# Attention over memory slots and two ReLU² MLPs on one core: the float64 weight conversion leaves GpSimd, and its first two pieces move to the front

## The chip, the cores and the metric

One core of a Trainium2 chip runs the whole program. The metric is the device time of one execution in microseconds (us), as the median of several runs. The engines are called PE (TensorE, matrix products; PEld is its weight load), DVE (VectorE), ACT (ScalarE), POOL (GpSimd) and SP (SyncE, which here issues nearly all DMAs).

## What is computed

Three stages follow one another: an attention whose keys and values are first pooled into 32 memory slots per head, and two MLPs with a squared ReLU.

```python
def _attn_ref(q, k, v, phi):                 # 8 batches, 8 heads, 576 tokens, 64 wide; phi: 32 slots
    a = np.exp(phi - np.max(phi, axis=2, keepdims=True))
    a = a / (np.sum(a, axis=2, keepdims=True) + 1e-09)
    k_m = np.einsum('bhsm,bhsd->bhmd', a, k)
    v_m = np.einsum('bhsm,bhsd->bhmd', a, v)
    scores = (1 / sqrt(64)) * np.matmul(q, k_m.transpose(0, 1, 3, 2))
    attn = softmax of scores over the 32 slots
    return np.matmul(attn, v_m)

def _moe_ref(x, w_in, w_out, s, b):          # x: 4608 x 512, w_in: 512 x 2048, w_out: 2048 x 512
    g = s * np.maximum(x @ w_in, 0.0) ** 2 + b
    return g @ w_out

def _moe2_ref(x, w_in, w_out):
    return np.maximum(x @ w_in, 0.0) ** 2 @ w_out
```

The four weight matrices (w_in1, w_out1, w_in2, w_out2) arrive as float64; all else is float32.

## The kernel before

**Order of the work.** Batch 0's attention runs first and alone. Then a list of steps `(b, half, f)` drives the first MLP: for one half batch (288 tokens) and one block `f` of 128 hidden units, `h1` makes the hidden block (6 products into `hps`, line 455, then ReLU, square and a high part `g[0]` on ACT, and the low part `g[1]` on DVE, line 464), two steps ahead of `x1`, which multiplies it by w_out1 (12 products into `acc`, line 472). The steps of one (b, half) share one accumulator; `SEGS` begins with batch 0's blocks 0 to 3, then 4 to 7, then batch 1's 0 to 7. Attention of the next batches and `v_fold` (slot values times w_in1, `vps`, line 424, split into high and low parts `vp` on lines 429 and 430) are generators that are advanced between the products. After the last batch a second phase computes the second MLP.

**Split operands.** Products that need more precision than one float32r pass are made of high and low parts: (high, high), (high, low), (low, high). So `x1` needs `g[0]`, `g[1]` and both parts of its piece of w_out1, and waits for the low part of w_out1 with the third product of each column block.

**The float64 conversion.** `narrow_later` lists pieces of 1024 KB: in the order two of w_in1 (kind "float"), two of w_out1 (kind "split"), and so on, 16 in all for the first MLP; the 16 of the second are of kind "spill" and come later. `narrow_load` issues a piece's DMA into a pool `w64` of two buffers (tile `wt`), with a lower priority for the scheduler than the code around it. `narrow` converts a piece of 128x1024 words: on ACT `wx` = high word as a float, scaled (line 119); on DVE a shift by 3 (line 120); for kind "float" ACT makes the sign (line 122), DVE puts the low word's top bits in (line 126) and POOL multiplies by the sign into the tile `w1` (line 129); for the other kinds DVE puts in the sign bit (line 124) and the low bits (line 126); "split" then has a high part on ACT (line 131) and a low part as a subtraction on POOL (line 132). Calls of `narrow` stand at three places of batch 0's attention (`FIRST`) and then at listed steps.

**Batch 0's attention.** `load_phi` and `load_kv` bring phi, k and v. DVE reduces phi to a maximum per partition (line 194, `pm`); two transposes on PE (lines 207, 216) with a reduction and a copy on DVE between them (lines 210, 213) spread it; DVE subtracts (line 221), ACT takes the exponential (line 223, `e`). `kvs` (line 239) is the pooled k and v; for batches 0 and 1 the sum of the weights is one small product per weight tile with `ones` (line 249), for the later batches DVE sums first (line 232, `es`) and two products follow (line 258). Then come the reciprocal `rs` (lines 267, 268), the scaled copies (lines 276, 277), transposes `kvt`, copies into `kb` (line 289), query transposes `qps` (line 305) and copies `qT`, scores `sp` (line 320), the softmax on DVE and ACT (lines 332 to 343: maximum `m_`, subtraction, exponential on ACT, sum `l_`, reciprocal, multiplication), transposed probabilities `pp` (line 348) and their high and low parts `pt` (lines 357, 358).

A scheduler orders each engine's instructions from priorities; each engine then runs its own in that order and waits on semaphores.

## Time and profile before

| | us |
|---|---|
| median of 3 runs | 1603.72 (1602.5 to 1604.74) |
| the profiled execution, its own time | 1603.0 |
| its span in the trace | 1601.2 |
| PE busy in the span | 1559.0 (97%) |
| ACT busy | 703.9 (44%) |
| DVE busy | 676.6 (42%) |
| POOL busy | 40.5 (3%) |

The shares are averages over very different stretches: of the 40 equal slices of the span, PE has 0.5 and 0.8 in the first two and 0.9 or more from the fifth on, while DVE is at 0.9 in the third. The profiled execution lies 0.7 us below the median of the runs and 1.8 us above its own span.

### The profile page before, as it was taken

Reading aid. Unit: us, or ns where it says so; the run is one execution under the profiler, and the core shown is the slowest. Engines: PE = TensorE matmul, PEld = TensorE weight load, DVE = VectorE, ACT = ScalarE, POOL = GpSimd, SP = SyncE. Lnnn points to the kernel's source line nnn. Section 1 sums busy time; section 2 is a strip of 40 time slices with the busy share of each in tenths; the row PEclk is TensorE's granted clock in tenths of the full one; section 3 lists DMA queues with packets and bytes.
Section 4 is the critical chain, followed back from the end, with each engine's and each line's share of the span. In section 5 each row is a group of like instructions: output and inputs, shape, how many; then the busy total and the mean of one; then the engine's idle time right before and its main releaser. Section 6 shows DMA issues by size and latency. Waiting matters only on the chain.

```text
span 1601.2 us, 25941 instructions
## 1 busy us (share of the span) xinstructions
PE 1559.0 (97%) x10872; PEld 1351.6 (84%) x10872; DVE 676.6 (42%) x1155; ACT 703.9 (44%) x1475; POOL 40.5 (3%) x23
## 2 busy tenths in 40 slices
PE   5889999999999999999999999999999999999998
PEld 3778899989999998989988888888888888888887
DVE  5796454645555564444253323232323223232222
ACT  3676555665666666567542322232222222232221
POOL 1323000000000000000000000000000000000000
PEclk8899999999999999999999999999999999999999
DMA  8655322425334441104040102010100101010100
GB/s 270 202 167 176 118 76 66 138 80 174 104 129 124 145 138 45 51 18 145 16 134 27 53 0 53 1 53 0 36 18 4 50 0 53 1 27 0 27 1 27
DMA packets 105300, 118.06 MB, mean 74 GB/s; under 512 B 42208, under 2 KB 82144, under 8 KB 105184
## 3 DMA queue, kind: packets, MB, share of 16 engines
q1 hardware_dynamic: 104864, 115.89, 23.4%
q8 instruction: 85, 1.39, 0.4%
q10 hardware_dynamic: 320, 0.52, 0.1%
q14 instruction: 31, 0.25, 0.1%
HBM read 86.77 MB, written 29.62 MB: 73 GB/s over the span
## 4 chain that ended last, share of the span: by engine, by line
PE 91%; DVE 4%; DMA 2%; ACT 1%; issue 1%; POOL 0%; SPq 0%; ACTq 0%; DVEq 0%
PE hps L676 25%; PE oacc L724 25%; PE acc L472 23%; PE hps L455 12%; PE vps L424 2%; PE sp L320 1%; PE kvs L239 1%; PE qps L305 1%; DMA kv<-in_v_dram 1%; DMA wt<-in_moe_w_out_dram 1%; DVE wx L126 1%; DVE wx L120 1%; PE pp L348 1%; DVE pm L194 1%; DVE wx L124 1%
## 5 line engine op out<-in xcount | busy, mean ns | idle before, releaser
L472 PE MATMUL acc<-g,wo 128*128 128x288 f32 (+1 forms) x3072 | 474.3, 300 | 8.9 <-ACT xo L501 3.4
L472 PEld LDWEIGHTS acc<-g,wo 128*128 128x128 f32 x3072 | 427.8, 190 | 37.7 <-issue 17.1
L724 PE MATMUL oacc<-wo,g 128*128 128x512 f32 x1728 | 419.6, 392 | 0.0
L724 PEld LDWEIGHTS oacc<-wo,g 128*128 128x128 f32 x1728 | 324.3, 188 | 73.4
L676 PE MATMUL hps<-xh,wi 128*128 128x512 f32 x1152 | 384.2, 394 | 0.0
L681 ACT ACTIVATE r<-hps 128x512 f32<-128x512 f32 x144 | 86.0, 597 | 462.4 <-PE hps L676 462.3
L682 DVE TENSOR_TENSOR r<-r 128x512 f32<-128x512 f32 x144 | 99.7, 692 | 445.8 <-ACT r L681 445.8
L676 PEld LDWEIGHTS hps<-xh,wi 128*128 128x128 f32 x1152 | 216.1, 188 | 49.5
L455 PE MATMUL hps<-pt,vp 128*128 128x288 f32 x1536 | 257.6, 301 | 0.3 <-ACT vp L429 0.3
L464 DVE TENSOR_TENSOR g<-r,g 128x288 fp32r<-128x288 f32 x256 | 125.9, 493 | 252.8 <-ACT g L463 250.4
L455 PEld LDWEIGHTS hps<-pt,vp 128*128 128x128 f32 x1536 | 221.5, 190 | 6.2 <-issue 4.3
L676 PE MATMUL hps<-xl,wi 128*128 128x512 f32 x576 | 225.4, 391 | 0.0
L461 ACT ACTIVATE r<-hps 128x288 f32<-128x288 f32 x256 | 105.4, 412 | 193.0 <-PE hps L455 190.6
L684 DVE TENSOR_TENSOR g<-r,g 128x512 fp32r<-128x512 f32 x144 | 99.6, 692 | 84.5 <-ACT g L683 84.5
L683 ACT CAST g<-r 128x512 fp32r<-128x512 f32 x144 | 89.5, 621 | 94.7 <-DVE r L682 93.6
L676 PEld LDWEIGHTS hps<-xl,wi 128*128 128x128 f32 x576 | 108.1, 188 | 25.1
L462 ACT ACTIVATE r<-r 128x288 f32<-128x288 f32 x256 | 113.8, 444 | 6.9
L463 ACT CAST g<-r 128x288 fp32r<-128x288 f32 x256 | 110.7, 432 | 7.1
L430 DVE TENSOR_TENSOR vp<-vps,vp 128x512 fp32r<-128x512 f32 x64 | 41.6, 685 | 12.4 <-ACT vp L429 12.1
L424 PE MATMUL vps<-w,vmT 64*32 64x512 f32 x512 | 39.3, 615 | 4.8 <-POOL w L129 4.6
L126 DVE SCALAR_TENSOR_TENSOR wx<-wt,wx 128x1024 int32<-128x1024 int32 x32 | 41.1, 1283 | 0.4
L429 ACT CAST vp<-vps 128x512 fp32r<-128x512 f32 x64 | 34.7, 587 | 13.3 <-PE vps L424 12.7
(225 smaller groups left out, 727.5 us busy)
## 6 DMA issues: line engine op xcount, KB each, us to landing
wt<-in_moe_w_in_dram SPq DMA_DIRECT2D x16, 1024.0 KB, 6.3
wt<-in_moe_w_out_dram SPq DMA_DIRECT2D x16, 1024.0 KB, 5.9
q<-in_q_dram SPq DMA_DIRECT2D x72, 128.0 KB, 3.3
x1d<-xo SPq DMA_DIRECT2D x16, 576.0 KB, 3.6
kv<-in_k_dram SPq DMA_DIRECT2D x23, 384.0 KB, 4.9
kv<-in_v_dram SPq DMA_DIRECT2D x23, 384.0 KB, 5.2
out_dram<-oo SPq DMA_DIRECT2D x68, 128.0 KB, 2.3
x<-x1d SPq DMA_DIRECT2D x6, 1024.0 KB, 5.5
```

What stands on the lines that cost most here:

```text
L455: nc.tensor.matmul(hps[:, :NB1], lhsT=w[:, wi], rhs=pt[xi][:, hp, t0:t0 + NB1], start=(i == 0), stop=(i == 5))
L461: nc.scalar.activation(r[:, :NB1], hps[:, :NB1], AF.Relu)
L462: nc.scalar.activation(r[:, :NB1], r[:, :NB1], AF.Square)
L463: st["act"] = nc.scalar.copy(g[0][:, :NB1], r[:, :NB1])
L464: nc.vector.tensor_tensor(out=g[1][:, :NB1], in0=r[:, :NB1], in1=g[0][:, :NB1], op=ALU.subtract)
L472: nc.tensor.matmul(acc[d][:, :n], lhsT=wo1[:, f, wi, d * P:d * P + P], rhs=g[xi][:, :n], start=(first and i == 0), stop=(store is not None ...
L676: nc.tensor.matmul(hps[:, :NB2], lhsT=w[:, wi], rhs=xs[i][xi][:, d], start=(n == 0), stop=(n == 3 * ND - 1))
L681: nc.scalar.activation(r, hps[:, :NB2], AF.Relu)
L682: nc.vector.tensor_tensor(out=r, in0=r, in1=r, op=ALU.mult)
L683: nc.scalar.copy(g[0], r)
L684: nc.vector.tensor_tensor(out=g[1], in0=r, in1=g[0], op=ALU.subtract)
L724: nc.tensor.matmul(acc[t], lhsT=g[xi][:, t * P:t * P + P], rhs=wo2[:, f, wi], start=(f == 0 and n == 0), stop=(f == NF - 1 and n == 2))
```

## The change

- Kind "float" no longer uses ACT's sign and POOL's multiplication: DVE puts in the sign bit as for the other kinds, and the instruction that puts in the low bits writes the result straight into `w1`. Kind "split" makes its low part on DVE instead of POOL.
- The DMAs of the first two pieces (both of w_in1) are issued at normal priority: the first right behind phi's, the second behind k and v and ahead of q. The calls of `narrow` in batch 0's attention stand at the generator's steps 4, 8 and 20 instead of 6, 12 and 22.
- Batch 0's weight sums go over DVE's `es` and two products, as for batches 2 and up; batch 1 alone keeps the small products.
- Batch 1's maximum over phi (`pm`) is ordered behind a low part `g[1]` of the first steps (`issue_after(st["dve"])`).

```diff
-    def narrow_load(n=1):
+    def narrow_load(n=1, later=30):
         for src, kind, dst in [narrow_todo.pop(0) for _ in range(min(n, len(narrow_todo)))]:
-            with tc.high_priority(-30):
+            with tc.high_priority(-later) if later else ExitStack():
...
                 nc.vector.tensor_scalar(out=x, in0=x, scalar1=3, scalar2=None, op0=ALU.logical_shift_left)
-                if kind == "float":
-                    nc.scalar.activation(dst[0], hw.bitcast(F32), AF.Sign)
-                else:
-                    nc.vector.scalar_tensor_tensor(out=x, in0=hw, scalar=-(1 << 31), in1=x,
-                                                   op0=ALU.bitwise_and, op1=ALU.bitwise_or)
-                nc.vector.scalar_tensor_tensor(out=x, in0=lw, scalar=29, in1=x,
+                nc.vector.scalar_tensor_tensor(out=x, in0=hw, scalar=-(1 << 31), in1=x,
+                                               op0=ALU.bitwise_and, op1=ALU.bitwise_or)
+                nc.vector.scalar_tensor_tensor(out=dst[0].bitcast(I32) if kind == "float" else x,
+                                               in0=lw, scalar=29, in1=x,
                                                op0=ALU.logical_shift_right, op1=ALU.bitwise_or)
-                if kind == "float":
-                    nc.gpsimd.tensor_tensor(out=dst[0], in0=xf, in1=dst[0], op=ALU.mult)
-                elif kind == "split":
+                if kind == "split":
                     nc.scalar.copy(dst[0], xf)
-                    nc.gpsimd.tensor_tensor(out=dst[1], in0=xf, in1=dst[0], op=ALU.subtract)
-                else:
+                    nc.vector.tensor_tensor(out=dst[1], in0=xf, in1=dst[0], op=ALU.subtract)
+                elif kind == "spill":
                     nc.sync.dma_start(dst[0], xf)
...
-        nc.vector.tensor_reduce(
-            out=pm.rearrange("p (n m) -> p n m", m=M),
-            in_=ph.rearrange("p n j m -> p n m j"), axis=AX.X, op=ALU.max)
+
+        with tc.issue_after(st["dve"].ins) if b == 1 else ExitStack():
+            nc.vector.tensor_reduce(
+                out=pm.rearrange("p (n m) -> p n m", m=M),
+                in_=ph.rearrange("p n j m -> p n m j"), axis=AX.X, op=ALU.max)
...
-            narrow_load(1)
+            narrow_load(1, 0)
...
-            if g == 0 and b > 1:
+            if g == 0 and b != 1:
...
-            if b < 2:
+            if b == 1:
...
-        for hp in range(2 if b > 1 else 0):
+        for hp in range(2 if b != 1 else 0):
...
-        nc.vector.tensor_tensor(out=g[1][:, :NB1], in0=r[:, :NB1], in1=g[0][:, :NB1], op=ALU.subtract)
+        st["dve"] = nc.vector.tensor_tensor(out=g[1][:, :NB1], in0=r[:, :NB1], in1=g[0][:, :NB1], op=ALU.subtract)
...
-    narrow_load(1)
+    narrow_load(1, 0)
...
-        if n in (6, 12, 22) and done < FIRST:
+        if n in (4, 8, 20) and done < FIRST:
```

How the order moves, at three places. Lines of the changed kernel differ: 121 and 123 are the sign bit and the low bits (before 124 and 126), 128 the low part of w_out1 (before 132 on POOL), 192 is `pm`, 208 and 211 the steps between the two transposes, 219 the subtraction, 230 `es`, 265 and 266 `rs`, 287 `kb`, 462 the low part `g[1]`.

SP's queue from the program's start, before:

```order
L169 DMA ph<-in_phi_dram 128x4x288
L178 DMA kv<-in_k_dram 128x4x192
L179 DMA kv<-in_v_dram 128x4x192
L178 DMA kv<-in_k_dram 128x4x192
L179 DMA kv<-in_v_dram 128x4x192
L178 DMA w_3_144<-in_k_dram 128x4x192
L179 DMA w_3_144<-in_v_dram 128x4x192
L185 DMA q<-in_q_dram 128x4x64 x6
L584 DMA s_sb<-in_moe_s_dram 128x1
L585 DMA b_sb<-in_moe_b_dram 128x1
L97 DMA wt<-in_moe_w_in_dram 128x2x512 x2
```

and now:

```order
L165 DMA ph<-in_phi_dram 128x4x288
L97 DMA wt<-in_moe_w_in_dram 128x2x512
L174 DMA kv<-in_k_dram 128x4x192
L175 DMA kv<-in_v_dram 128x4x192
L174 DMA kv<-in_k_dram 128x4x192
L175 DMA kv<-in_v_dram 128x4x192
L174 DMA w_3_144<-in_k_dram 128x4x192
L175 DMA w_3_144<-in_v_dram 128x4x192
L97 DMA wt<-in_moe_w_in_dram 128x2x512
L181 DMA q<-in_q_dram 128x4x64 x6
```

The first piece of w_in1 goes ahead of all six k and v transfers and the second ahead of q's; both were behind all of these, and behind the two small broadcasts.

DVE from the maximum over batch 0's phi on, before (`mx` and `mxb` are the reduction and the copy between the two transposes):

```order
L194 TENSOR_REDUCE pm<-ph 128x128
L210 TENSOR_REDUCE mx<-t_196 128x2
L213 COPY mxb<-mx 128x128
L221 TENSOR_TENSOR ph<-ph,t_202 128x4x96 x3
L267 TENSOR_SCALAR rs<-kvs 128x1 x2
L268 RECIPROCAL rs<-rs 128x2
L289 COPY kb<-kvt 64x4x32 x2
L332 TENSOR_REDUCE m__448<-sp 128x12
L120 TENSOR_SCALAR wx<-wx 128x1024
```

and now, from behind the same maximum:

```order
L120 TENSOR_SCALAR wx<-wx 128x1024
L208 TENSOR_REDUCE mx<-t_196 128x2
L121 SCALAR_TENSOR_TENSOR wx<-wt,wx 128x1024
L211 COPY mxb<-mx 128x128
L123 SCALAR_TENSOR_TENSOR w_0_141<-wt,wx 128x1024
L219 TENSOR_TENSOR ph<-ph,t_202 128x4x96 x3
L230 TENSOR_REDUCE es<-e 128x128
L265 TENSOR_SCALAR rs<-kvs 128x1 x2
L266 RECIPROCAL rs<-rs 128x2
L120 TENSOR_SCALAR wx<-wx 128x1024
L121 SCALAR_TENSOR_TENSOR wx<-wt,wx 128x1024
L287 COPY kb<-kvt 64x4x32
```

The first piece's three DVE instructions now stand between the steps of the maximum, the second piece's around the copies into `kb`; before, both pieces stood behind these, among the softmax.

DVE from behind the low part `g[1]` of the second step, with the third group's softmax, to the low part of the second piece of w_out1, now:

```order
L337 TENSOR_REDUCE l__495<-e 128x12
L338 TENSOR_SCALAR l__495<-l__495 128x12
L339 RECIPROCAL l__495<-l__495 128x12
L120 TENSOR_SCALAR wx<-wx 128x1024
L341 TENSOR_TENSOR e<-e,l__495 128x384
L121 SCALAR_TENSOR_TENSOR wx<-wt,wx 128x1024
L462 TENSOR_TENSOR g_2_158<-r,g_2_157 128x288
L123 SCALAR_TENSOR_TENSOR wx<-wt,wx 128x1024
L356 TENSOR_TENSOR pt_315<-pp,pt_314 128x192
L462 TENSOR_TENSOR g_0_154<-r,g_0_153 128x288
L192 TENSOR_REDUCE pm<-ph 128x128
L128 TENSOR_TENSOR wo_116<-wx,wo_116 128x2x512
```

Before, this low part was POOL's, and batch 1's maximum stood much earlier, behind the first softmax group's multiplication:

```order
L343 TENSOR_TENSOR e<-e,l__456 128x384
L194 TENSOR_REDUCE pm<-ph 128x128
L339 TENSOR_REDUCE l__460<-second 128x12
L358 TENSOR_TENSOR pt_386<-pp,pt_385 128x192
L340 TENSOR_SCALAR l__460<-l__460 128x12
```

The maximum now stands directly ahead of the low part of w_out1, behind the first low parts `g[1]`.

## Rows read from the trace of the kernel before

**Rows 1.** Busy time by stretch: PE, PEld, DVE, ACT, POOL, granted clock, DMA share, GB/s.

```profile
50.00:150.00 100.00, 85.74 (x904) 76.37 (x905) 85.49 (x124) 71.95 (x147) 32.99 (x14) 0.93 0.61 201
150.00:1601.00 1451.00, 1443.71 (x9537) 1253.68 (x9536) 564.17 (x990) 612.00 (x1286) 0.00 (x0) 1.00 0.20 59
```

**Rows 2.** The chain that ended last, from 0 to 60 us: start, length, what.

```profile
26.45 2.21 DVE wx L120
...
30.64 2.53 DVE e L343
...
33.21 0.90 PE pp L348 x3
...
55.12 2.42 POOL wo L132
```

**Rows 3.** POOL's timeline: one of its 16 conversion instructions.

```profile
48.16 2.38 POOL L132 TENSOR_TENSOR wo<-wx,wo 128x1024 fp32r<-128x1024 f32 x1 [15.42 <-ACT wo L131]
```

**Rows 4.** DVE's timeline: instructions with nothing on POOL, and (48.45) one beside POOL.

```profile
24.39 1.22 DVE L126 SCALAR_TENSOR_TENSOR wx<-wt,wx 128x1024 int32<-128x1024 int32 x1
...
38.70 0.68 DVE L120 TENSOR_SCALAR wx<-wx 128x1024 int32<-128x1024 int32 x1
...
40.93 0.35 DVE L358 TENSOR_TENSOR pt<-pp,pt 128x192 fp32r<-128x192 f32 x1
...
48.45 2.41 DVE L464 TENSOR_TENSOR g<-r,g 128x288 fp32r<-128x288 f32 x1 [2.40 <-ACT g L463]
...
51.92 0.44 DVE L464 TENSOR_TENSOR g<-r,g 128x288 fp32r<-128x288 f32 x1
```

**Rows 5.** DVE's groups by line, 20 to 150 us: count | busy us, mean ns | idle before.

```profile
L464 DVE TENSOR_TENSOR g<-r,g 128x288 fp32r<-128x288 f32 x27 | 21.6, 805 | 5.4 <-ACT g L463 5.4
L126 DVE SCALAR_TENSOR_TENSOR wx<-wt,wx 128x1024 int32<-128x1024 int32 x16 | 21.5, 1347 | 0.2
L120 DVE TENSOR_SCALAR wx<-wx 128x1024 int32<-128x1024 int32 x16 | 15.4, 960 | 3.6 <-ACT wx L119 3.6
L124 DVE SCALAR_TENSOR_TENSOR wx<-wt,wx 128x1024 int32<-128x1024 int32 x8 | 11.8, 1479 | 0.1
...
L343 DVE TENSOR_TENSOR e<-e,l__1040 128x384 f32<-128x384 f32 x1 | 2.4, 2367 | 0.0
L340 DVE TENSOR_SCALAR l__1134<-l__1134 128x12 f32<-128x12 f32 x1 | 2.1, 2082 | 0.0
```

**Rows 6.** DMA issue at 4.94 us, the last of k and v: count, size, us to landing.

```profile
w<-in_v_dram SPq DMA_DIRECT2D x1, 384.0 KB, 6.2
```

**Rows 7.** Timeline, 0 to 24 us: start, length, engine, line, operation [idle before].

```profile
4.77 2.08 DVE L194 TENSOR_REDUCE pm<-ph 128x128 f32<-128x1152 f32 x1 [3.90 <-DMA ph<-in_phi_dram]
4.94 0.99 SPq L179 DMA_DIRECT2D w<-in_v_dram  x1
...
9.77 1.57 PE L239 MATMUL kvs<-kv,e 64*32 64x128 f32 x39 [1.20 <-ACT e L223]
...
17.67 0.23 DVE L267 TENSOR_SCALAR rs<-kvs 128x1 f32<-128x1 f32 x2 [7.58 <-PE kvs L249]
...
20.90 1.19 ACT L119 ACTIVATE wx<-wt 128x1024 f32<-128x1024 f32 x1
...
21.89 0.92 PE L320 MATMUL sp<-kb,qT 128*64 128x64 f32 x24 [0.85 <-DVE kb L289]
```

**Rows 8.** PE's timeline, 50 to 147 us: products that had to wait.

```profile
50.92 2.98 PE L472 MATMUL acc<-g,wo 128*128 128x290 f32 x20 [1.32 <-DVE g L464]
...
57.59 0.54 PE L472 MATMUL acc<-g,wo 128*128 128x290 f32 x2 [1.26 <-POOL wo L132]
...
70.75 1.02 PE L239 MATMUL kvs<-kv,e 64*32 64x128 f32 x47 [1.95 <-DMA kv<-in_v_dram]
...
144.46 3.25 PE L472 MATMUL acc<-g,wo 128*128 128x288 f32 x12 [3.44 <-ACT xo L501]
```

**Rows 9.** The page's costliest groups: busy us, mean ns of one | idle before, releaser.

```profile
L684 DVE TENSOR_TENSOR g<-r,g 128x512 fp32r<-128x512 f32 x144 | 99.6, 692 | 84.5 <-ACT g L683 84.5
```

## The prediction

> **What bounds the kernel now.** I read the busy time by stretch first: from 150 us to the end PE is busy for 1443.7 of 1451 us at the full clock (2.4 GHz), and from 50 to 150 us for only 85.7 of 100 us, at a mean granted clock of 0.93 [rows 1]. So nearly all that this change can win or lose lies in the first 150 us; behind that, PE's own products set the pace, and a shift of the whole is kept to the end. In that stretch the reader should see that POOL is busy for 33 us, all of it the conversion, and DVE for 85.5.
>
> The chain of waits from 0 to 60 us tells who is late there: DVE's conversion (26.45), a softmax multiplication (30.64), and then the low part of w_out1 on POOL (55.12) [rows 2]. PE waits for these: the first transposed probabilities start at 33.21 [rows 2], the first product with a low `g` at 50.92, the first with w_out1's second low part at 57.59 [rows 8].
>
> The groups on DVE then show something odd, the same instruction at two lengths. The shift takes 0.68 alone and 2.21 beside POOL [rows 4, 2], the low part `g[1]` 0.44 alone and 2.41 at 48.45, while POOL's instruction runs from 48.16 for 2.38 [rows 4, 3]. The excess over the lone length, from the means between 20 and 150 us: line 464 27 x (0.805 - 0.44) = 9.9, line 126 16 x (1.347 - 1.22) = 2.0, line 120 16 x (0.96 - 0.68) = 4.5, line 124 8 x (1.479 - 1.22) = 2.1, the two long multiplications of line 343 2.53 + 2.37 less twice 0.59 (0.44 x 384/288, an estimate) = 3.7, the long one of line 340 (12 elements) some 1.9 [rows 4, 5, 2]. Sum: 24 us that DVE stands still beside POOL's 16 instructions.
>
> **The change part by part.** *POOL's work on DVE.* Eight w_in1 pieces get one more DVE instruction like line 126 (1.22 [rows 4]): 9.8 us. Eight low parts of w_out1, 1024 elements wide with two inputs: at least 1.22, as that row of the same width, at most 2 x 0.69 = 1.38, as two of 512 [rows 9]; I take 1.3, so 10.4. `es` is a reduction like `pm`, 2.1 [rows 7]. Against these 22.3 stand the 24 us of standing still. In all a draw; what counts is where they lie. ACT loses eight signs of about 1.2 each (as line 119 [rows 7]), off the path.
>
> *What comes earlier.* Two w_in1 pieces are converted by about 21.5 us, where DVE mostly waited. So behind 20 us DVE loses 2 x (0.68 + 1.22) = 3.8 and the 24, and gains 6 x 1.22 + 8 x 1.3 = 17.7: 10 us less work up to the last conversion. This is one account of the gain: 10 us, if DVE's idle time stays as it was.
>
> *The second account follows the start.* phi lands at 4.77, the last of k and v at 4.94 + 6.2 = 11.1 [rows 7, 6]: 6 x 384 KB in 6.4 us, in the order of issue, 360 KB per us. A megabyte ahead of them costs 2.8. So the first piece lands at 7.6, k and v end at 14.0, the second piece at 16.8, q behind it by 19. DVE now meets the first piece's shift right behind `pm`: 7.6 + 1.2 (ACT) + 0.7 = 9.5, where `pm` ended at 6.9, a delay of 2.6; two more conversion instructions stand in the maximum's way, 2.4 less the transposes that they cover, say 1.4. So `kvs` starts 4.0 later than 9.77, at 13.8, when k and v have come. Its 72 products (39 took 1.57) need 2.9; the 72 small ones are gone, and `es` (exponentials done at 14.8, plus 2.1) is ready at 16.9: `rs` at 17.2 against 17.67 [rows 7]. ACT then takes the second piece (to 18.0) ahead of the scaled copies, and DVE's three instructions for it stand around the copies into `kb`, which end at about 21.6. The scores start at 21.8 against 21.89 [rows 7]: up to here nothing is won.
>
> Then it comes. From the scores to the first `pp`, DVE had two shifts and two low-bit instructions in the way and two stalls: 0.68 + 1.22 + 2.21 + 1.22 + (2.53 - 0.59) = 7.3 [rows 2, 4]. All gone: `pp` at 25.9. To the last low part `pt` (40.93 + 0.35 = 41.28 [rows 4]) `pm` leaves, -2.1, and the first w_out1 piece's low-bit instruction, which stood behind it, comes ahead of it, +1.2: 8.2 earlier, at 33.1. To the first product with a low `g` the 2.0 of stalling at 48.45 goes [rows 4], and the scores that stood between the `hps` products are done before, about 1 (an estimate): 11.2 earlier, 39.7 against 50.92.
>
> Here some is given back. The second piece of w_out1 now has its low part on DVE, and batch 1's maximum stands directly ahead of it. Before, that product came 6.7 later (57.59 - 50.92 [rows 8]). Now DVE's queue from the second `g[1]` to there holds the third softmax group (about 1.5), the shift, two conversion instructions, two `g[1]`, one `pt`, `pm` and the low part: 1.5 + 0.68 + 2.44 + 0.88 + 0.35 + 2.1 + 1.3 = 9.2 [rows 4, 7]. Less overlap, some 8.7: 48.5 against 57.59, so 9 us earlier. This wait is the next thing that is late.
>
> Behind that point DVE gains 6 x 1.22 + 6 x 1.3 = 15.1 and loses 24 - (1.5 + 1.9 + 2.0) = 18.6, another 3.5 in its favour. But I count only 1 of it: POOL is gone from the waits, while k and v of batch 1 (1.95 late at 70.75) are asked for by PE sooner [rows 8], the products stand in longer blocks of one kind, and each low part now holds up the `g[1]` behind it. SP's queue carries the same transfers, the q and w_out1 loads some 4 us sooner.
>
> *The clock.* After 3.44 us without work 12 products took 3.25 at 144.46, where 20 took 2.98 at 50.92 [rows 8]: 1.5 us lost. The new wait ahead of 48.5 can cost the same once, or the old ones fall away; I put it at 0 and in the range. The Trainium skill, in "TensorE: Matmul & The Clock Gate", Part 1, says that the slow clock is the default and that activity releases it; by that rule the longer empty stretch before `kvs` and the wait ahead of 48.5 would both be paid, and my gain would be 8.5 instead of 10.
>
> Sum: -9 to 57.59, -1 behind it, -10; both accounts agree. Against the profiled execution (1603.0) that is 1593.0; its time is 0.7 below the median of the runs, so **1593.7**.
>
> **The rivals.** *DVE becomes the bound (slower).* If the long instructions are not long because of POOL, nothing comes back: DVE's work behind 48.5 grows by 15.1, and with DVE at 85 of 100 us [rows 1] and in front of each `g[1]`, PE waits for it. Time: -9 + 15.1 = +6, **1609.7**. It decides as soon as less than 6 of the 18.6 us return. Against it: the 2.41 at 48.45 ends within 0.4 of POOL's end (50.54), and instructions of 0.44 and 2.41 differ in nothing else [rows 3, 4]. The Trainium skill, "SBUF — State Buffer", Who interferes with whom, goes further: DVE and GpSimd share a port pair as an exclusive lock, and the later one blocks fully. By that rule up to 16 x 2.4 = 38 us could be lost to it; the rows show 24, since not every DVE instruction beside POOL needs the pair.
>
> *The gain is given back before 150 us.* The 9 us hold at 48.5 and PE then waits anew: batch 1's k and v (2 more), low parts in front of `g[1]` (13 pieces, 0.5 each by an estimate from 1.3 less the 0.8 that two steps' lead still covers), one half-clock stretch (1.5) [rows 4, 8]. With half of this the change is at -9 + 5 = -4, with all of it at +1: 1599.7 to 1604.7, **1602** in the middle. For it: DVE's queue is the longest in that stretch. Against: its work shrinks there.
>
> *More than forecast.* PE idles 14.3 of the 100 us [rows 1]. If the 3.5 of DVE and the 3.44 at 144.46, whose cause is the conversion chain, go too: -16, **1587.5**.
>
> *The change does not do what it says.* The first piece lands late, its DMA being of another shape than k and v: each us of it delays `pm`'s successors by one, from the point where `rs` passes 17.7. With 3 us late the front loses 3 (1597), which lies within the range.
>
> **How the numbers follow.** Forecast (gain of 6 to 13): 0.60, its own range 1590 to 1598. Given back (gain of 0 to 6): 0.20. More (gain above 13): 0.12. Slower: 0.08. About 0.2% (3.2 us) is what a measurement of this kernel can tell from no change. Of "given back" half lies above 3.2 us of gain, so faster 0.60 + 0.12 + 0.10 = 0.82; same 0.11; slower 0.07, the rest of the slower case. The range 1586 to 1602 leaves out the slower case, some of "given back" and the end of "more".
>
> **What would show it.** Right: no POOL row behind 2 us; lines 120, 462 and 341 at 0.68, 0.44 and 0.55 throughout; the first piece landed near 7.6 and `kvs` from about 13.8; scores near 21.8; the first `pp` near 26; the first low-`g` product near 40; the third product of the second w_out1 piece near 48.5, held by DVE's line 128 behind `pm`; PE dense from 135 to 140 us instead of 147. Wrong: `kvs` or the scores later than 24, so that the front eats its own gain; DVE above 95% and PE waiting on line 462 between 50 and 130 us; a granted clock below 0.9 there.

## The result and the profile after

The change took the kernel from 1603.28 to **1581.88 us** (1581.76 to 1583.42), a ratio of 0.9868 [0.9851, 0.9885]: 21.4 us, twice the forecast and below its range. On another occasion the same kernel took 1581.60.

By stretch (columns as in [rows 1]), the kernel after:

```profile
50.00:150.00 100.00, 93.50 (x1007) 81.24 (x1006) 75.80 (x129) 69.25 (x154) 0.00 (x0) 0.98 0.59 198
150.00:1581.00 1431.00, 1423.76 (x9378) 1235.55 (x9370) 559.02 (x980) 600.45 (x1257) 0.00 (x0) 1.00 0.19 59
```

PE is busy for 93.5 instead of 85.7 us of the 100, DVE for 75.8 instead of 85.5, POOL not at all. From 150 us to the end PE again stands still for only 7.2 us. So the reader should see that all of the gain is made by 150 us.

The start, from the timeline (start, length, what, idle before):

```profile
7.35 1.12 ACT L119 ACTIVATE wx<-wt 128x1024 f32<-128x1024 f32 x1 [4.66 <-DMA wt<-in_moe_w_in_dram]
...
12.87 3.01 PE L237 MATMUL kvs<-kv,e 64*32 64x128 f32 x87 [1.67 <-ACT e L221]
...
17.95 0.22 DVE L265 TENSOR_SCALAR rs<-kvs 128x1 f32<-128x1 f32 x2 [1.99 <-PE kvs L256]
...
22.02 0.34 PE L318 MATMUL sp<-kb,qT 128*64 128x64 f32 x4 [1.46 <-DVE kb L287]
...
27.34 0.52 PE L346 MATMUL pp<-ident,e 128*128 128x128 f32 x3 [1.95 <-DVE e L341]
...
33.58 0.35 DVE L356 TENSOR_TENSOR pt<-pp,pt 128x192 fp32r<-128x192 f32 x1
...
37.22 0.83 DVE L462 TENSOR_TENSOR g<-r,g 128x288 fp32r<-128x288 f32 x2 [1.10 <-ACT g L461]
...
46.80 0.67 PE L470 MATMUL acc<-g,wo 128*128 128x290 f32 x3 [0.34 <-DVE wo L128]
```

DVE's groups from 20 to 150 us, against [rows 5]:

```profile
L121 DVE SCALAR_TENSOR_TENSOR wx<-wt,wx 128x1024 int32<-128x1024 int32 x15 | 18.3, 1221 | 0.2
L462 DVE TENSOR_TENSOR g<-r,g 128x288 fp32r<-128x288 f32 x35 | 15.5, 453 | 15.7 <-ACT g L461 15.7
L128 DVE TENSOR_TENSOR wo<-wx,wo 128x1024 fp32r<-128x1024 f32 x8 | 9.8, 1222 | 0.7 <-ACT wo L127 0.7
...
L120 DVE TENSOR_SCALAR wx<-wx 128x1024 int32<-128x1024 int32 x14 | 9.7, 693 | 6.5 <-ACT wx L119 6.5
```

Every lengthened instruction is gone: the low part `g[1]` takes 0.453 in the mean instead of 0.805, the shift 0.693 instead of 0.960. The last column counts as much: DVE now stands 15.7 us ahead of the `g[1]`, waiting for ACT, where it was 5.4; it has become early.

**Where the 21.4 us were won.** Two places can be found in both traces: the first transposed probabilities of batch 1, and a folding of V with w_in1 behind the last conversion. PE's timeline before:

```profile
91.87 0.55 PE L348 MATMUL pp<-ident,e 128*128 128x128 f32 x3 [2.53 <-DVE e L343]
...
120.22 1.82 PE L472 MATMUL acc<-g,wo 128*128 128x288 f32 x12 [1.71 <-DVE xo L497]
...
164.11 1.09 PE L424 MATMUL vps<-w,vmT 64*32 64x512 f32 x16
```

and after:

```profile
80.29 0.52 PE L346 MATMUL pp<-ident,e 128*128 128x128 f32 x3
...
143.84 1.09 PE L422 MATMUL vps<-w,vmT 64*32 64x512 f32 x16
```

At the first place 11.6 us are won, at the second 20.3; over the whole spans of the two traces it is 19.6 (1601.2, 1581.6), since the profiled execution of the kernel after was the slowest of its four, 1583.42. So the stretch between the two places is shorter by **8.7**; the forecast had 1 for all that comes behind 57.59. Busy time of just this stretch (columns as in [rows 1]), before:

```profile
91.87:164.11 72.24, 66.09 (x503) 60.33 (x503) 52.94 (x77) 48.43 (x99) 17.80 (x7) 0.93 0.47 155
```

and after:

```profile
80.29:143.84 63.55, 61.84 (x483) 54.37 (x484) 47.25 (x82) 43.58 (x94) 0.00 (x0) 0.97 0.53 179
```

PE stood still for 6.2 us and now for 1.7 (4.4 of the 8.7): the waits of 1.71 and of 3.44 at 144.46 [rows 8] are gone. Its busy time fell by the other 4.3, with the mean clock from 0.93 to 0.97. Not all of that is gain: up to the second place both kernels have done the same 576 products of `x1` and `h1`, but up to the first the kernel after has done 204 of them and the kernel before 185. The 19 that moved ahead are worth some 2.5 us (an estimate: 18 of them take 2.39 in the kernel before, from 151.29 to 153.68). The rest, some 1.8, fits the half clock: PE runs at 1.2 GHz for 10.2 us of the stretch before (92.6 to 96.0 and 143.8 to 150.6) and for 3.4 after (99.9 to 103.3). So like for like this stretch gave some 6.2 us and the part ahead of it some 14. The wait of 2.53, gone too, lies just ahead of the stretch.

### The profile page after: what moved, and what is told of

Same layout as the page of the kernel before. It is cut to its first block, busy times and chain, and to the rows that moved or that the text cites. A ratio compares the mean times of both kernels' runs of the same rounds, so it can differ in the third digit from the quotient of the medians.

```text
span 1581.6 us, 25635 instructions
## 1 busy us (share of the span) xinstructions
PE 1548.0 (98%) x10732; PEld 1341.6 (85%) x10732; DVE 672.2 (43%) x1172; ACT 694.9 (44%) x1467; POOL 1.0 (0%) x7
## 4 chain that ended last, share of the span: by engine, by line
PE 93%; DVE 3%; DMA 2%; ACT 1%; issue 1%; SPq 0%; ACTq 0%; DVEq 0%
PE hps L674 25%; PE oacc L722 25%; PE acc L470 24%; PE hps L453 12%; PE vps L422 2%; PE sp L318 1%; PE kvs L237 1%; PE qps L303 1%; DMA kv<-in_v_dram 1%; DMA wt<-in_moe_w_in_dram 1%; DVE pm L192 1%; PE pp L346 0%; DMA ph<-in_phi_dram 0%; DMA x<-x1d 0%; DVE wx L121 0%
## 5 line engine op out<-in xcount | busy, mean ns | idle before, releaser
L470 PE MATMUL acc<-g,wo 128*128 128x288 f32 (+1 forms) x3072 | 468.6, 298 | 0.5 <-DVE wo L128 0.3
L470 PEld LDWEIGHTS acc<-g,wo 128*128 128x128 f32 x3072 | 423.2, 188 | 27.6 <-issue 13.5
L462 DVE TENSOR_TENSOR g<-r,g 128x288 fp32r<-128x288 f32 x256 | 116.2, 456 | 246.0 <-ACT g L461 243.5
L428 DVE TENSOR_TENSOR vp<-vps,vp 128x512 fp32r<-128x512 f32 x64 | 41.7, 685 | 12.0 <-ACT vp L427 11.6
L119 ACT ACTIVATE wx<-wt 128x1024 f32<-128x1024 f32 x32 | 36.8, 1151 | 11.0 <-DMA wt<-in_moe_w_in_dram 9.4
```

The source lines that it names most:

```text
L462: st["dve"] = nc.vector.tensor_tensor(out=g[1][:, :NB1], in0=r[:, :NB1], in1=g[0][:, :NB1], op=ALU.subtract)
L470: nc.tensor.matmul(acc[d][:, :n], lhsT=wo1[:, f, wi, d * P:d * P + P], rhs=g[xi][:, :n], start=(first and i == 0), stop=(store is not None ...
```

## The experiments

All times are against the kernel before, run beside each.

| run | median us | ratio [95%] |
|---|---|---|
| conversion alone (conv_only) | 1590.96 | 0.9921 [0.9906, 0.9936] |
| all but the conversion (rest_only) | 1585.84 | 0.9895 [0.9877, 0.9913] |
| early pieces alone (early_only) | 1594.46 | 0.9950 [0.9933, 0.9967] |
| without early pieces (no_early) | 1587.04 | 0.9897 [0.9882, 0.9912] |
| without the sum on DVE (no_es) | 1586.16 | 0.9891 [0.9877, 0.9906] |
| maximum not ordered (no_pm) | 1584.24 | 0.9880 [0.9860, 0.9901] |
| last eight pieces only (late_conv) | 1596.22 | 0.9957 [0.9942, 0.9972] |
| after + 15 on GpSimd (pool_shadow) | 1592.72 | 0.9933 [0.9919, 0.9948] |
| after + 15 on DVE (dve_shadow) | 1584.71 | 0.9885 [0.9871, 0.9900] |
| the same, first in the queue (dve_now) | 1595.86 | 0.9951 [0.9936, 0.9965] |
| before + products (warm_before) | 1602.62 | 0.9990 [0.9978, 1.0001] |
| after + 5 products (warm_after) | 1580.97 | 0.9860 [0.9844, 0.9877] |
| after + 8 products (warm_after8) | 1582.45 | 0.9875 [0.9859, 0.9892] |
| after once more (after_again) | 1581.60 | 0.9868 [0.9853, 0.9883] |
| after + earlier k, v (kv2) | 1583.50 | 0.9876 [0.9861, 0.9891] |

### The parts of the change, one by one

Conversion alone, on the kernel before (the new lines of `narrow`, and nothing else):

```diff
-                    nc.gpsimd.tensor_tensor(out=dst[1], in0=xf, in1=dst[0], op=ALU.subtract)
+                    nc.vector.tensor_tensor(out=dst[1], in0=xf, in1=dst[0], op=ALU.subtract)
...
```

> The kernel before with the conversion alone taken off GpSimd; loads, conversion steps, the first batch's small products and the maximum of batch 1 stay as they were. The whole change measured -21.4 us: some -11.6 by the first transposed probabilities of batch 1, and another -8.7 from there to the last product group of that stretch. Theory A (the second part comes from GpSimd no longer blocking DVE, so it is there without the early loads): -12 to -16 us against the kernel before, the waits of 1.7 and 3.4 us on ACT's and DVE's xo gone, the stretch from the first pp of batch 1 to the v_fold vps as long as after the change (63.5 us) within 2. Theory B (the second part comes from the head start of the two early pieces, which puts less conversion work behind 80 us): -3 to -8 us, that stretch near 70 us or more. Theory C (DVE's added work is worth what its stalls cost, the draw of the prediction): 0 to -3 us.

All but the conversion, on the kernel after (the old `narrow` again):

```diff
+                if kind == "float":
+                    nc.gpsimd.tensor_tensor(out=dst[0], in0=xf, in1=dst[0], op=ALU.mult)
...
```

> The changed kernel with the old conversion put back (signs on ACT, the multiplication and the low part of w_out1 on GpSimd); everything else of the change stays. Theory A: DVE is blocked as before, so only the start is won: -4 to -8 us against the kernel before, and the stretch behind the first pp of batch 1 is near the 72.1 us of before. Theory B: -14 to -20 us, that stretch near 64 us.

The early pieces alone, on the kernel before:

```diff
-            narrow_load(1)
+            narrow_load(1, 0)
...
-        if n in (6, 12, 22) and done < FIRST:
+        if n in (4, 8, 20) and done < FIRST:
```

> The kernel before with the early loads and the conversion steps 4, 8 and 20 alone; GpSimd still multiplies, 144 small products for the sums, maximum as before. Taking the early part out of the changed kernel cost 5.2 us. Theory B (head start is the main thing): -6 to -12 against before. If it only pays together with the summed exponentials, because both pieces delay the first kvs products by 3 to 4 us and the small products then stand in front of the scores: 0 to -5. The half-clock stretch may stay or go; by the run with added products it makes no more than 1 us.

The kernel after with this edit undone:

> The changed kernel with the first two pieces of w_in1 loaded and converted where the kernel before had them (loads of lower priority, steps 6, 12 and 22); conversion without GpSimd, the summed exponentials and the ordered maximum stay. The conversion alone gave -12.3, everything but the conversion -17.5, all of it -21.4. Theory B (head start): most of the rest is lost, -10 to -14 against the kernel before, with the half-clock stretch between 27 and 48 us back. Theory A (conversion): -17 to -21.

Conversion alone gave -12.3, all but it -17.4, the early pieces alone -9.0; taking the early pieces out of the change cost 5.2, taking the conversion out only 4.0. The parts overlap: neither theory A nor B, as put, explains the whole. The length of the stretch between the two places above, on which the theories were staked, sorts them for each part by itself: 72.2 us before, 72.2 with the early pieces alone (81.35 to 153.54), 62.2 with the conversion alone (87.59 to 149.83), 66.5 with all but the conversion (80.20 to 146.70), 63.6 after. So the conversion alone is enough for the second part, as theory A has it, and the early pieces alone bring none of it; but A's forecast for all but the conversion, near 72.1, failed. The early pieces alone gave the -9 of the prediction's walk through the start, although that walk contains the other parts too; their trace has the second stretch as it was. PE's waits from 80 to 150 us there (total us, times, longest):

```profile
PE acc L472 <- ACT xo L501: 3.2, 1, 3.2
PE pp L348 <- DVE e L343: 2.4, 2, 1.8
PE acc L472 <- DVE xo L497: 1.6, 1, 1.6
```

These are the three waits of the kernel before, some 10 us sooner. A head start only shifts them.

In the run with all but the conversion they are gone although GpSimd works as before. DVE's group for the low part `g[1]` there, 80 to 150 us:

```profile
L466 DVE TENSOR_TENSOR g<-r,g 128x288 fp32r<-128x288 f32 x24 | 18.5, 781 | 16.3 <-ACT g L465 16.3
```

and the two lengthened groups from 20 to 150 us:

```profile
L466 DVE TENSOR_TENSOR g<-r,g 128x288 fp32r<-128x288 f32 x34 | 26.1, 778 | 19.5 <-ACT g L465 19.5
...
L120 DVE TENSOR_SCALAR wx<-wx 128x1024 int32<-128x1024 int32 x14 | 11.2, 800 | 5.2 <-ACT wx L119 5.2
```

The blocking is still in the length (781 ns), but it fell on instructions that were 16.3 us early. Against the means of the kernel after it is 34 x (0.778 - 0.453) + 14 x (0.800 - 0.693) = 12.5 us, and yet this run is only 4.0 slower than the kernel after. What brought that order about was not separated further: it is the scheduler's answer to the sums, the maximum and the early pieces together.

Without batch 0's sum on DVE, and with the maximum left to the scheduler, on the kernel after:

```diff
-            if g == 0 and b != 1:
+            if g == 0 and b > 1:
...
-        with tc.issue_after(st["dve"].ins) if b == 1 else ExitStack():
+        with ExitStack():
```

> The changed kernel with the 72 small products of batch 0 put back in place of the sum on DVE and its two products; nothing else undone. The prediction counted the sum at 2.1 us of DVE in a place where DVE mostly waits, and the small products at their time on PE, both ahead of the scores. If PE is the later one there: 1 to 3 us slower than the changed kernel (-18.5 to -20.5). If DVE is the later one: 0 to 2 us faster (-21.5 to -23.5). The stretch behind the first pp of batch 1 should not change by more than 0.5 us.

> The changed kernel with batch 1's maximum free to go where the scheduler puts it (as in the kernel before) and nothing else undone. If the maximum, which now stands directly ahead of the second w_out1 piece's low part, costs what the prediction put there (2 us given back), and no other place costs it: 2 us faster than the changed kernel, -23. If it goes back to its old place ahead of the last transposed probabilities, it delays the first product with a low g by 2.1 and the kernel is 0 to 2 us slower than the changed one: -19.5 to -21.5. If it makes no difference on the path: -21 to -22.

The sum is worth some 4.3 us, more than the 1 to 3 expected (the two intervals just touch): PE was the later one, the scores began at 26.26 instead of 22.02. The maximum stays unsettled: four runs at 1581.5 twice and at 1587.0 and 1587.5. That its place costs 2 us, as the prediction had it, is not borne out.

### Where the second part came from

The kernel before, with the new conversion from the ninth piece on:

```diff
+            new = done_n[0] > 8
...
-                    nc.gpsimd.tensor_tensor(
+                    (nc.vector if new else nc.gpsimd).tensor_tensor(
```

> The kernel before, in which only the last eight of the sixteen pieces (converted from about 85 us on) are converted without GpSimd; start, loads and the first eight pieces are as before, and PE's order is the same up to there. Between 80 and 144 us the changed kernel won another 8.7 us beyond its start, where the prediction counted 1. Theory A (GpSimd's blocking of DVE in that stretch, with its waits of 2.5, 1.7 and 3.4 us): -5 to -9 us against the kernel before, the 3.44 wait on ACT's xo gone, the last folding of V with w_in1 from 164 to about 156 to 159 us. Theory B (the head start of the early pieces carries it): 0 to -2 us, since nothing here starts sooner and eight instructions of 1.22 us are added to DVE. If only the low parts' latency counts: -2 to -4.

It gave -7.3, with nothing sooner before 85 us: the first transposed probabilities of batch 1 start at 91.80 (before 91.87), and the folding at 154.52 instead of 164.11. Busy time from 80 to 150 us, the kernel before:

```profile
80.00:150.00 70.00, 61.20 (x482) 54.45 (x481) 61.73 (x86) 50.99 (x106) 22.54 (x9) 0.93 0.58 188
```

and this run:

```profile
80.00:150.00 70.00, 68.55 (x555) 60.53 (x554) 58.18 (x99) 51.80 (x113) 3.43 (x1) 1.00 0.59 199
```

In the same 70 us PE works for 7.4 us more, DVE for only 3.6 less. How little of DVE's time can hold up so much of PE's is seen at the longest wait. The timeline of the kernel before, all engines:

```profile
138.47 3.18 POOL L132 TENSOR_TENSOR wo<-wx,wo 128x1024 fp32r<-128x1024 f32 x1 [6.32 <-ACT wo L131]
...
139.45 3.28 DVE L126 SCALAR_TENSOR_TENSOR wx<-wt,wx 128x1024 int32<-128x1024 int32 x1
...
142.76 1.04 ACT L131 CAST wo<-wx 128x1024 fp32r<-128x1024 f32 x1 [3.12 <-DVE wx L126]
...
144.02 0.39 ACT L501 COPY xo<-acc 128x288 f32<-128x288 f32 x1
```

DVE's low-bit instruction, 1.22 alone, meets POOL's subtraction and takes 3.28. ACT's cast of the piece waits for it, and behind that cast in ACT's queue stand copies that empty PE's accumulators. So PE, which has nothing to do with this piece, waits 3.44, and then runs 12 products in 3.25 us at half clock [rows 8], where the same 12 took 1.78 (the row at 128.97 of the early-pieces run below). The wait and the slow products behind it hold PE up by some 4.9 us (3.44 + 3.25 - 1.78). The block of 2.1 us on DVE accounts for 2.1 of the wait at most; some 1.4 would have been left. Behind a wait of 1.71, at 120.22, 12 products took 1.82, so the half clock may well belong to the block too, but that is argued and not shown. The early-pieces run has the same picture 9.8 us sooner:

```profile
128.70 3.19 POOL L132 TENSOR_TENSOR wo<-wx,wo 128x1024 fp32r<-128x1024 f32 x1 [6.04 <-ACT wo L131]
128.97 1.78 PE L472 MATMUL acc<-g,wo 128*128 128x288 f32 x12
129.68 3.29 DVE L126 SCALAR_TENSOR_TENSOR wx<-wt,wx 128x1024 int32<-128x1024 int32 x1
```

### What a blocked microsecond of DVE costs, and what a worked one

The kernel after with one GpSimd multiplication behind each of the first 15 pieces, for which nothing waits; then the same on DVE; then on DVE at the front of its queue:

```diff
+                if kind != "spill" and narrow_todo:
+                    d = dst[0] if kind == "float" else dst[0].bitcast(F32)
+                    nc.gpsimd.tensor_tensor(out=wo1[:, NF - 2:, 1, :], in0=d, in1=d, op=ALU.mult)
```

```diff
-                    nc.gpsimd.tensor_tensor(
+                    nc.vector.tensor_tensor(
```

```diff
+                    with tc.high_priority(400):
```

> The changed kernel with 15 GpSimd multiplications of 128 x 1024 added, one behind each of the first 15 converted pieces, reading the converted piece and writing to the low part of w_out1's last pair, which is written properly later. Nothing waits for them, and the order of every other instruction on every engine is that of the changed kernel. The prediction held GpSimd responsible for 24 us of lengthened DVE instructions beside 16 such instructions. If so, the lengthened instructions come back: lines 462, 120 and 341 (0.44, 0.69, 0.55 us each) show means well above these between 20 and 150 us, the excess summing to 15 to 30 us, and the kernel is 4 to 12 us slower than the changed one. If that time is hidden behind PE (DVE idles for 24 of 100 us): the same excess, but under 2 us slower. If the lengthening came from sharing the data and not from GpSimd running at all: no excess and the same time.

> The changed kernel with 15 multiplications of 128 x 1024 added on DVE (1.22 us each, 18 us in all), one behind each of the first 15 converted pieces, reading the converted piece and writing to the low part of w_out1's last pair. With the same multiplications on GpSimd, DVE's instructions grew by 14 us and the kernel by 10.8 over the changed one. If DVE's time counts the same whether it works or is blocked: 18 x 10.8 / 14, some 14 us slower than the changed kernel, -7 against before. If the conversion's own instructions find DVE's idle time (it idles for 24 us between 50 and 150) and a blocked one does not: 2 to 7 us slower, -14 to -19. The scheduler places the added ones itself, so some rows around them move.

> As the run with 15 multiplications added on DVE, but each is put at the front of DVE's queue as soon as its piece is there, ahead of the softmax, the low parts of g and the low part of w_out1, as a blocked DVE would be; left to the scheduler they cost 2.8 us for 18 us of DVE, while 14 us of blocking by GpSimd cost 10.8. If it is the place (a blocked instruction can be any, the scheduler puts added work where it hurts least): 6 to 14 us slower than the changed kernel, -8 to -15 against before. If it is the kind (a blocked DVE holds something else up besides itself, or the scheduler's place hardly matters): 2 to 5 us slower, as before, -16 to -19.

DVE's groups with the GpSimd multiplications, 20 to 150 us:

```profile
L121 DVE SCALAR_TENSOR_TENSOR wx<-wt,wx 128x1024 int32<-128x1024 int32 x15 | 18.8, 1252 | 0.2
L128 DVE TENSOR_TENSOR wo<-wx,wo 128x1024 fp32r<-128x1024 f32 x8 | 17.2, 2144 | 0.9 <-ACT wo L127 0.9
L465 DVE TENSOR_TENSOR g<-r,g 128x288 fp32r<-128x288 f32 x31 | 15.3, 505 | 7.9 <-ACT g L464 7.9
L120 DVE TENSOR_SCALAR wx<-wx 128x1024 int32<-128x1024 int32 x14 | 12.9, 924 | 4.1 <-ACT wx L119 3.9
...
L344 DVE TENSOR_TENSOR e<-e,l__974 128x384 f32<-128x384 f32 x1 | 2.0, 1995 | 0.0
```

Against the kernel after, behind 20 us: 8 x (2.144 - 1.222) + 14 x (0.924 - 0.693) + 31 x (0.505 - 0.453) + 15 x (1.252 - 1.221) + (1.995 - 0.557) = 14.1 us of blocking, a little below the 15 to 30 expected. The kernel is 10.8 slower: 0.77 us for each us. Its instruction order on DVE and on every other engine is that of the kernel after, so nothing but GpSimd's work and the blocking differs. This price holds for this order of the queues: in the run with all but the conversion 12.5 us of blocking came back, some 19.5 us of DVE's work (16 x 1.22) went, and the cost was 4.0, where the two prices of this section give some 7 (an estimate).

The same 15 on DVE are 15 x 1.22 = 18.3 us of work, and cost 2.8 (its interval overlaps that of the kernel after): 0.15 for each us. Put at the front of the queue they cost 14.3 against the kernel after of the same occasion, just above the 6 to 14 expected: 0.78. Then PE waits for DVE at the transposed probabilities as it did before the change (PE's waits, 20 to 150 us):

```profile
PE pp L350 <- DVE e L345: 6.0, 2, 3.9
```

So the place is enough to make DVE's time dear. The same work in the scheduler's order goes where DVE would have stood idle; one reading is that a blocked DVE is like work put in front of whatever comes next. That the kind adds nothing is not shown: both runs with work on DVE moved rows on PE and ACT too, and the agreement of 0.78 with 0.77 is a coincidence in part. At the front of the queue PE runs at half clock for much longer. Busy time from 20 to 150 us there:

```profile
20.00:150.00 130.00, 112.91 (x1097) 96.95 (x1098) 114.09 (x185) 81.76 (x180) 0.00 (x0) 0.86 0.63 206
```

The kernel after and the other two runs have a mean clock of 0.96 in this stretch. Over the whole span PE is busy for 9.1 us more than in the kernel after of the same occasion (1556.8, 1547.7), most of the 14.3; with the GpSimd multiplications it is busy for only 2.5 more than in the kernel after (1550.5, 1548.0), and most of the 10.8 is PE standing still.

### The clock

The kernel before with products that nobody reads, 14 behind the scores and 10 behind the first folding; in the kernel after, 5 and 8 behind the folding alone:

```diff
+        with tc.issue_after(pe.ins):
+            for _ in range(n):
+                st["pe"] = nc.tensor.matmul(t[:, :P], lhsT=ident, rhs=ident, start=True, stop=True)
```

> The kernel before with 24 products of the identity with itself added on PE, written to a PSUM bank that nothing reads: 14 behind the first scores and 10 behind the first folding of V with w_in1, both places where PE stands idle. The order of every other instruction on every engine is that of the kernel before. In the kernel before PE ran at half clock from 27.8 to 48.1 us, with PE busy for 14.8 us of it. Theory D (the clock: a good part of the change's gain is that PE has no longer such an empty start, so that this stretch shrinks from 20 to 7 us): the stretch goes or shortens to under 10 us, the last product ahead of the first acc at 48.9 comes 3 to 5 us sooner, and the kernel is 3 to 6 us faster than before. Rival E (PE only waits for DVE and POOL there, the clock is a by-product): the first low-g product stays within 1 us of 50.9 and the kernel within 1.5 us of before, or slower by what the added products delay.

> The changed kernel with 5 products of the identity with itself behind the first folding of V with w_in1 (PE idles for 1.95 us there, at 25.4), written to a PSUM bank that nothing reads; the order of everything else is that of the changed kernel. In it PE ran at half clock from 28.3 to 35.0 us, which by the rows costs 2.9 us of PE. Theory D (clock): that stretch moves later or goes, 1 to 3 us faster than the changed kernel. Rival E (PE would wait for DVE instead): within 1 us of it.

> The changed kernel with 8 instead of 5 products of the identity with itself behind the first folding. With 5, PE's half-clock time before 50 us went from 2.9 to 0 by the rows, and the time from 1581.9 to 1581.0. If the clock is worth anything beyond the noise there: 0.5 to 2 us faster than the changed kernel in the same call. If DVE's chain sets the pace: within 0.5 us, or slower by up to 1, since 8 products reach past the moment when the first transposition is ready.

> The changed kernel once more, unchanged, on the chip of the two runs beside it, so that they are compared with it and not with its time on another occasion: 1581 to 1584 us, -20 to -22.

Busy time from 28 to 48 us: the kernel before, the same with the added products, and the kernel after:

```profile
28.00:48.00 20.00, 15.28 (x70) 9.05 (x71) 15.18 (x23) 7.72 (x16) 2.45 (x2) 0.50 0.73 247
```

```profile
28.00:48.00 20.00, 14.64 (x100) 9.90 (x100) 16.65 (x24) 9.02 (x19) 4.20 (x3) 0.83 0.74 245
```

```profile
28.00:48.00 20.00, 16.90 (x110) 13.98 (x110) 18.54 (x34) 12.39 (x27) 0.00 (x0) 0.83 0.82 266
```

The added products gave the kernel before the same mean clock as the change did, 0.83 instead of 0.50 (0.50 is 1.2 GHz throughout, 0.83 is 2.4 GHz for two thirds of the stretch), and the time is not told apart from before (0.9990, with 1 inside the interval; at most 3.5 us by its lower end). The trace is of the fastest of its ten executions, 1598.59. Up to the first product with a low `g` 1.95 us were won (48.97 against 50.92, the row below), and there PE waits for DVE more than before:

```profile
48.97 1.21 PE L481 MATMUL acc<-g,wo 128*128 128x290 f32 x7 [1.62 <-DVE g L473]
```

So in the start, where DVE sets the pace, rival E is the nearer one, though it allowed only 1 us there; theory D had 3 to 5, and 3 to 6 at the end. In the kernel after, 5 products gave 0.9 less (against its time on another occasion) and 8 gave 0.9 more than the kernel itself, both within each other's intervals: nothing that can be told.

### One wait of the kernel after

The third part of batch 1's k and v loaded with the first two:

```diff
-        if b == 0 and g > 1:
+        if b < 2 and g > 1:
...
-        for g in range(NJG if b == 0 else 2):
+        for g in range(NJG if b < 2 else 2):
```

> The changed kernel, in which the third part of batch 1's k and v is loaded with the first two, into the place in w_in1's last part that batch 0's used, instead of waiting for a buffer. In the changed kernel PE waits 2.30 us for it at 59.5, the longest wait it has left behind 50 us. If that wait lies on the path: 1 to 2.5 us faster than the changed kernel, -22.5 to -24. If DVE's chain (batch 1's softmax) sets the pace there, or the sooner transfer delays phi and the pieces behind it in the queue: within 1 us of the changed kernel, or slower by up to 2.

The wait of 2.30 went, and the kernel took 1583.5, 1.6 more than the kernel after and within the intervals the same. The wait was not simply worth nothing: PE now stood still for 1.82 at 56.89, ahead of the same part of the sums, with no releaser in the profile, and the first folding of V behind it came at 60.37 instead of 65.16:

```profile
60.37 2.42 PE L422 MATMUL vps<-w,vmT 64*32 64x512 f32 x16 [0.92 <-ACT vn L275]
```

But these 16 products, which take 1.55 in the kernel after, ran at half clock, as all of PE did from 58.8 to 65.6, where the kernel after has the full clock. The transposed probabilities of batch 1 came at 81.30 instead of 80.29. So what was won was lost again by then; that the half clock is part of the loss can be read, what the rest is stays open. No version here is told apart from the kernel after on the better side.

## Why the prediction was wrong

The sign was right and the first nine of its ten us nearly so (10.8), the size of the whole was not.

- **The start.** Forecast and trace: first piece landed 7.6, 7.35; `kvs` 13.8, 12.87; `rs` 17.2, 17.95; scores 21.8, 22.02; first `pp` 25.9, 27.34; last `pt` done 33.1, 33.93; first low `g` 39.7, between 37.6 and 38.1 (the two subtractions at 37.22); third product of the second w_out1 piece 48.5, 46.80, held as forecast by the low part on line 128, which stood right behind `pm`. There -9 was forecast and 57.59 [rows 8] less 46.80 is 10.8, with 12 more products of `x1` and `h1` already done (64, 52). The early pieces alone measured -9.0, without the other parts that the walk through the start contains, so the agreement of these two numbers is luck.
- **A slip in it.** "Its 72 products (39 took 1.57) need 2.9" mixes the program's products with the rows' counts: the 14 products added behind the scores show as x28 in the timeline, so 39 in a row are only half as many products. `kvs` took from 12.87 to `rs` at 17.95, some 5, not 3.4; it began 0.9 sooner than forecast, which hid the slip.
- **The step that failed** is "Behind that point DVE gains 6 x 1.22 + 6 x 1.3 = 15.1 and loses 24 - (1.5 + 1.9 + 2.0) = 18.6, another 3.5 in its favour. But I count only 1 of it". Behind that point 9.5 came by the folding (20.3 less 10.8), some 8 without the 12 products done ahead of it, and the run with the last eight pieces measured 7.3 by itself. The 3.5 was not far off as DVE time: between the two places DVE is busy for 5.7 us less (52.94, 47.25). Wrong was the price: added and blocked us were set against each other one for one, as in "In all a draw". The conversion alone, worth about nothing by that draw, measured -12.3. The runs put 0.15 on an added us and 0.77 on a blocked one; by these, 18.6 blocked us gone are worth 14.3 and 15.1 added cost 2.3, some 12 (an estimate from the two runs, too high against the 8 to 9.5 measured; nothing waited for the added multiplications, while products wait for the added conversion work). The sentence "what counts is where they lie" was right and was not carried through to the waits.
- **The rival that came nearest** was "More than forecast", -16 (its 1587.5 is 0.2 low: 1603.7 less 16 is 1587.7). It named the right wait (3.44 at 144.46) and its cause, but took DVE's 3.5 at face value and left out the 2.53 at 91.87 and the 1.71 at 120.22. At 0.12 its chance was too small: the trace of the kernel before shows a lengthened instruction of DVE ahead of each of the three waits (2.37 at 89.44, 3.29 at 113.34, 3.28 at 139.45).
- **"DVE becomes the bound"** fell: DVE is busy for 75.8 of the 100 us. "Given back" fell too: from the folding of V at 164.11 and at 143.84 to the end of the span it is 1437.1 and 1437.8 us, so only 0.7 was lost behind it.
- **What the instructions cost** held: the low part on line 128 took 1.22 (I took 1.3), `es` ran beside other work. That GpSimd was the cause of the long instructions is shown by the added multiplications. The Trainium skill, "SBUF — State Buffer", Who interferes with whom, says that the two share a port pair as an exclusive lock: who issues first has it for the whole instruction, and the other blocks. The trace agrees: DVE's 3.28 at 139.45 ends 1.1 us behind POOL's end at 141.65, and alone it takes 1.22 [rows 4].
- **The clock** was put at 0. For the start that held as a time: it rose from 0.50 to 0.83 between 28 and 48 us, and the run that raised it alone won nothing that can be told. Behind 80 us the half clock went with the waits ahead of it and is some 1.8 of the 8.7; there 0 was too little. In all PE ran at 1.2 GHz for 34 us of the first 165 before the change and for 10 after it. The rule of the Trainium skill that the prediction weighed ("TensorE: Matmul & The Clock Gate", Part 1) was read there as a cost of 1.5 for new waits; the trace shows the reverse, fewer empty stretches and less half clock behind them.

## What to carry to other kernels

Work added to an engine's queue and time in which another engine blocks it are not the same currency: price the first by the engine's idle time at that place, the second by the wait it ends on. Follow each lengthened instruction down the queues to the next wait of the bounding engine; it can end at an engine and a tile that have nothing to do with it. No price is a constant: 14.1 us of blocking cost 10.8 in one order of the queues, and in another 12.5 cost 4.0, net of 19.5 us of DVE's work that went with them. And where another engine sets the pace, raising the clock with filler buys little: at most 3.5 us here.

## What the runs showed of the hardware that was not expected

- GpSimd multiplications of 128 x 1024 that only read what DVE and ACT had finished lengthened DVE's instructions by 14.1 us, beside 14 of them behind 20 us; the other way, GpSimd's own took 1.89 us at the least and up to 2.87.
- 24 products that nobody reads raised the mean clock from 0.50 to 0.83 between 28 and 48 us, and the median of ten executions is not told apart from before (ratio 0.9990).
- Taking away a wait of 2.30 us on PE (the k and v load) won nothing: the folding behind it came 4.8 us sooner, and 6.8 us at half clock followed. A wait of 3.44 held PE up by 4.9 with the slow products behind it. The length of a wait alone did not tell.
